# Row statistics in one pass, gate products in another space, an earlier load and refitted planner times in a gated convolution and token-MLP kernel

## The chip, the cores and the metric

The kernel runs on one core of a Trainium2 chip. The metric is the device time of one launch in microseconds, as the median of several runs. The core has five engines with queues of their own: PE (matmul; PEld is its weight load), DVE (vector), ACT (scalar), POOL, and SP, which here only issues DMAs. Each queue runs in order; semaphores connect them.

## The reference

The inputs are bf16; S = 2048 rows, D = 640 channels, F = 1536 hidden units.

```python
x = A_q
g = sigmoid((x * gate_w).sum(-1, keepdims=True))
# A: short convolution (4 taps) over k, product with v, long causal convolution by FFT
k_shift = sum over t of k_pad[:, t:t+S, :] * shift_k[:, ks-1-t]
kv = k_shift * v
y = irfft(rfft(kv, 2S) * rfft(ssm_k, 2S))[:S] + kv * ssm_D
a = x * y
# B: layernorm over D without weights, MLP over the row (token) axis
h = (x - mean) / sqrt(var + 1e-5)
u = gelu_tanh(einsum("bsd,sf->bdf", h, w1) + b1)
b = (einsum("bdf,fs->bds", u, w2) + b2) transposed back
return g * a + (1 - g) * b
```

## The kernel before

The long convolution is done as transforms by matmul. A 2048-row sequence is held as `[128, 2, 4, 640]` halves: four residues p modulo 4, two blocks kt (`hk = 2h + kt` counts the four quarters of 512 rows). The forward transforms of the filter (`transp` through PE into `wT`, then `fwd` with the table `FTB`, results evacuated by ACT into `C[0]`, `C[1]`) and of kv (into `C[2]`, `C[3]`) are followed by additions and subtractions on DVE (`mixing`) that combine the residues. DVE then multiplies spectra (`cross`, `y1`, `product`), some sums being made by accumulating DMAs issued from POOL (`v1mix`, `acc_dma`). `invmix` undoes the mixing, and `inverse(h, Z)` transforms back with the table `GTB`, which is `FTB` transposed by four DMA transposes. ACT scales the inverse by the gate `gg` into `cgb`, DVE multiplies it by q (`q_hi` for the upper half of the rows, `q_lo` for the lower), adds it to `O1` and SP stores the rows.

The MLP has two products. `X` holds all of q, normalised in place: per row tile two `bn_stats` over 320 columns and one `bn_aggr` (`ln_tile`), then `ln_apply(hk)` for each quarter: on POOL var + 1e-5 into `vtmp` and its power of -0.5 into `rstd`, on DVE four `tensor_scalar` that subtract the mean and multiply. The first product ("m1", 12 hidden tiles ft of 32 matmuls each, weights in `ring`) fills PE wherever the convolution leaves it free and ends in a Gelu on ACT into `GT`. The second ("m2", 16 row tiles of 24 matmuls, weights in `W2`, an alias of `ring`) is the filler of the later part; ACT puts it into `O1`, which lies on `X`.

The gate is recovered from the normalised rows: DVE multiplies X by `gate_w` (`gq`, two row tiles each, three buffers), ACT sums each row (`gsum`, a copy into `junk` with an accumulator), and a few 16-column operations on DVE put mean and deviation back, `vtmp * rstd` being the standard deviation.

Buffers share space by hand: `gq` and `junk` lie on `KF` (the taps of the short convolution, read by PE until the fourth quarter's kv), `kp1` (one of two buffers for the permuted k that the k transposes read) lies on `GTB`, `q_hi` on `C[0]`, `q_lo` on half of `C[1]`, `cgb` on `FTB`, `W2` on `ring`.

The order of all work is set by a list scheduler in the file (`_Sched`). Each operation is added with an engine, an estimated duration, and a priority (its place in the program unless given; lower goes first; m1 and m2 have the highest numbers and so fill). The scheduler simulates the engines with these estimates, takes on each engine the ready operation of lowest number, and the order so found is what each engine's queue is given. PSUM has four tiles; at most three go to the convolution and two to the MLP. DMAs are modelled as one channel with 2 us of latency. An operation added with `.after` may not start ahead of another's start in this simulation. At run time only the order remains, with waits on semaphores wherever a dependence crosses engines.

L293 is the matmul helper, L617 `tensor_tensor`, L627 and L628 `tensor_scalar`, L655 `activation`, L724 the k copy, L845 and L847 the statistics, L260, L262 and L267 the DMA helper (transposing, accumulating, plain).

Of the kernel before, what the change touches and what calls it, by code (L numbers as in the profile page):

```python
# [322 lines left out]
class _Sched:  # L323
# [58 lines left out]
    def run(self):  # L382
# [24 lines left out]
        t = 0.0  # L407
# [4 lines left out]
        while started < n:  # L412
            while frees and frees[0][0] <= t:
                _, sl, cls = heapq.heappop(frees)
                nfree.append(sl)
                held[cls] -= 1
            nxt = []
            progress = False
            for e in engs:
                while pend[e] and pend[e][0][0] <= t:  # L420
                    _, p, i = heapq.heappop(pend[e])
                    heapq.heappush(ready[e], (p, i))
                if free[e] > t:
                    nxt.append(free[e])
                    continue
                skipped = []
                pick = None
                while ready[e]:
                    p, i = heapq.heappop(ready[e])
                    op = ops[i]  # L430
                    if op.vt is not None and op.vt.slot is None:
                        c = op.vt.cls
                        if not nfree or held.get(c, 0) >= self.limit.get(c, 99):
                            skipped.append((p, i))
                            continue
                    pick = op
                    break
                for s in skipped:
                    heapq.heappush(ready[e], s)
                if pick is None:  # L440
                    if pend[e]:
                        nxt.append(pend[e][0][0])
                    continue
                op = pick
                progress = True
                started += 1
                if op.vt is not None and op.vt.slot is None:
                    nfree.sort()
                    op.vt.slot = nfree.pop(0)
                    held[op.vt.cls] = held.get(op.vt.cls, 0) + 1  # L450
                op.start = t
                if e in ("SP", "QA") or op.lat < 0:
                    issue = 0.1
                    s = max(t + issue, dma_free)
                    dma_free = s + op.dur
                    op.end = dma_free + 2.0
                    free[e] = t + issue
                else:
                    op.end = t + op.dur
                    free[e] = op.end  # L460
                order.append(op)
                if op.vt is not None:
                    op.vt.left -= 1
                    if op.vt.left == 0:
                        heapq.heappush(frees, (op.end + 0.05, op.vt.slot, op.vt.cls))
                for s in op.asucc:
                    avail[s] = max(avail[s], op.start)
                    s.ndep -= 1
                    if s.ndep == 0:
                        heapq.heappush(pend[s.eng], (avail[s], s.prio, s.idx))  # L470
                for s in op.succ:
                    lat = 0.08 if s.eng == e else 0.15
                    if e == "PE" and s.eng == "PE":
                        lat = 0.0
                    avail[s] = max(avail[s], op.end + lat)
                    s.ndep -= 1
                    if s.ndep == 0:
                        heapq.heappush(pend[s.eng], (avail[s], s.prio, s.idx))
                nxt.append(free[e])
            if not progress:  # L480
                c = [x for x in nxt if x > t]
                if frees:
                    c.append(frees[0][0])
                assert c, "schedule stuck: " + str([(o.name, o.eng, o.ndep) for o in ops if not hasattr(o, "end")][:12])
                t = min(c)
# [19 lines left out]
def _build(nc, A_q, A_k, A_v, A_shift_k, A_ssm_k, A_ssm_D, B_x, B_w1, B_b1, B_w2, B_b2, gate_w, out):  # L505
# [10 lines left out]
    with ExitStack() as es:  # L516
# [32 lines left out]
            return bass.AP(tensor=h, offset=p0 * row + off, ap=[[row, pn]] + [list(d) for d in dims])  # L549

        gwb = alloc("gwb", [128, D], BF16)
        Drow = alloc("Drow", [1, D], BF16)
        ident = alloc("ident", [128, 128], BF16)
        KF = alloc("KF", [128, NG, 7, 32], BF16)
        cw = alloc("cw", [128, NG, 7], BF16)
        m32 = alloc("m32", [128, 32], BF16)
# [4 lines left out]
        vtmp = alloc("vtmp", [128, 16], F32)  # L561
# [18 lines left out]
        dif = alloc("dif", [128, 128], I32, at=base_of(SS) + 64 + 1024)  # L580
        dif2 = alloc("dif2", [128, 32], I32, at=base_of(SS) + 64 + 1536)
        KT = [alloc(f"KT{i}", [128, NG, KTW], BF16) for i in range(2)]
        gq = [alloc(f"gq{i}", [128, 2, D], BF16, at=base_of(KF) + 2560 * i) for i in range(3)]
        junk = alloc("junk", [128, D], BF16, at=base_of(KF) + 7680)
        ssm = alloc("ssm", [128, ND, S], BF16, at=base_of(C[3]))
        wT = alloc("wT", [128, 4, 4, D], BF16, at=base_of(C[2]))
        vkv0 = alloc("vkv0", [128, 2, 4, D], BF16, at=base_of(C[3]))
# [8 lines left out]
        O1 = alloc("O1", [128, 4, 4, D], BF16, at=base_of(X))  # L596
        tm = [alloc(f"tm{i}", [128, 2, 4, D], BF16, at=E_base + 2 * SL * 2 * i) for i in range(2)]
        q_lo = alloc("q_lo", [128, 2, 4, D], BF16, at=base_of(C[1]) + 2 * SL * 2)
        q_hi = alloc("q_hi", [128, 2, 4, D], BF16, at=base_of(C[0]))
        cgb = [alloc(f"cgb{i}", [128, 2, D], BF16, at=base_of(FTB) + 2560 * i) for i in range(3)]  # L600

        def n_of(ap):
# [3 lines left out]
            return n  # L606

        def dve_dur(n, mode):
            return n / {1: 960.0, 2: 1920.0, 4: 3840.0}[mode] + (0.1 if mode == 4 else 0.16)

        def act_dur(n, nap=0):
            return n / 1200.0 + 0.19 + 0.09 * nap

        def tt(eng, o, a, b, op, mode=2, prio=None):
            n = n_of(o)
# [49 lines left out]
            return SC.add(eng, 0.2, lambda s: T.op(eng, lambda e: e.memset(ap, val), [], [ap]), [], [ap], prio=prio)  # L665

        def mms(vt, items, prio=None, name="mm"):
            dur = sum(max(n_of(r) / 2400.0, 0.06) for _, _, r, _, _ in items)
            rd = []
            for _, l, r, _, _ in items:  # L670
                rd += [l, r]
# [48 lines left out]
        def k_turn(hk):  # L720
            o, i = kp[hk % 2], kn[hk % 2]
            ov = o[:, :, :].rearrange("p g (q c) -> p g q c", q=4)
            iv = V(i, 0, [[32, NG], [D, 4], [1, 32]])
            SC.add("DVE", 0.85, lambda s: T.op("DVE", lambda e: e.tensor_copy(ov, iv), [i[:, :, :]], [o[:, :, :]]), [i[:, :, :]], [o[:, :, :]], prio=0, name="kperm")  # L724
# [115 lines left out]
        def ln_tile(hk, p):  # L840
            t = 4 * hk + p
            xs = X[:, hk, p, :]
            for ci in range(2):
                o, i = stats[:, t, 6 * ci:6 * ci + 6], xs[:, 320 * ci:320 * ci + 320]
                SC.add("DVE", 0.46, (lambda o, i: lambda s: T.op("DVE", lambda e: e.bn_stats(o, i), [i], [o]))(o, i), [i], [o])  # L845
            o, i = mv[:, t, :], stats[:, t, :]
            SC.add("DVE", 0.2, (lambda o, i: lambda s: T.op("DVE", lambda e: e.bn_aggr(o, i), [i], [o]))(o, i), [i], [o])  # L847
# [84 lines left out]
        for ft in range(FT):  # L932
# [12 lines left out]
                mms(vt, items, prio=10 ** 6 + 4 * ft + hk, name="m1")  # L945
            g_ = act(GT[:, ft, :].rearrange("p (a b) -> p a b", a=2), two, ACT.Gelu_apprx_tanh, bias=cc[:, 16 + ft:17 + ft], vt=vt, prio=0, name="gelu")
            if ft == 0:
                act(junk[:, :], gwb[:, :], ACT.Copy, acc=gws[:, :], name="gws").after.add(g_)
# [12 lines left out]
        tt("DVE", gpre[:, :], gpre[:, :], gth[:, :], ALU.add, mode=1, prio=0)  # L961
        act(gth[:, :], gpre[:, :], ACT.Tanh, scale=0.5, prio=0)
# [4 lines left out]
        def w2_load(hk):  # L967
            for a in range(2):
                dma(W2[hk % 2][:, 6 * a:6 * a + 6, :], dr(B_w2, a * 6 * 128 * S + 512 * hk, [[S, 128], [128 * S, 6], [1, 512]]), 128 * 6144)

        for p in range(4):
            dma(GTB[:, p, :, :, :, :].rearrange("q a b c d -> q (a b c) d"), FTB[:, p, :, :, :, :].rearrange("q a b c d -> q (a b c) d"), 128 * 2048, rate=200.0, transpose=True, prio=10 ** 5)

        HORD = (2, 3, 0, 1)
        for n_, hk in enumerate(HORD):
            w2_load_at = n_
            W2h = W2[n_ % 2]
            for a in range(2):
                dma(W2h[:, 6 * a:6 * a + 6, :], dr(B_w2, a * 6 * 128 * S + 512 * hk, [[S, 128], [128 * S, 6], [1, 512]]), 128 * 6144)
            for p in range(4):  # L980
                vt = _VT("mlp")
                t = 4 * hk + p
# [170 lines left out]
```

## Time and profile before

| | |
|---|---|
| median of 3 runs | 198.19 us (197.91 to 199.74) |
| the profiled execution | 197.93 us, span 196.1 us, granted clock 0.996 |
| PE busy | 177.4 us, 1403 matmuls |
| DVE busy | 177.0 us, 196 instructions |
| ACT busy | 118.5 us, 187 instructions |
| POOL busy | 28.6 us, 30 instructions |
| DMA | 37.62 MB, mean 192 GB/s |

The span runs from the first to the last instruction of the profiled execution. Rows of a timeline begin with start and duration in microseconds, then engine, line, operation, output and inputs, and in brackets how long the engine stood idle ahead of it and what ended that. SPq is the time in which SP's queue issued a DMA. Rows with bars are groups: busy time, mean nanoseconds of one, idle time ahead.

### The profile page before, as it was taken

The numbers are of one execution on the slowest core, as the hardware profiler recorded it, in microseconds if no ns is written. First come the engines' busy times: TensorE is split into PE (matmuls) and PEld (weight loads), VectorE is DVE, ScalarE is ACT, GpSimd is POOL, SyncE is SP. The second block draws the span as 40 slices with busy tenths as digits, with TensorE's granted clock in tenths as the row PEclk, the third lists the DMA queues.
The fourth block names the chain that finished last, engine by engine and source line by source line (L and its number), as shares of the span: only waits on it lengthen the run. The fifth ranks groups of instructions, "written<-read, shape, count | busy, mean of one in ns | idle before, by whom it ended". The sixth has DMA issues, their size and how long they took to land.

```text
span 196.1 us, 3370 instructions
## 1 busy us (share of the span) xinstructions
PE 177.4 (90%) x1403; PEld 131.4 (67%) x1403; DVE 177.0 (90%) x196; ACT 118.5 (60%) x187; POOL 28.6 (15%) x30
## 2 busy tenths in 40 slices
PE   0759987999999999999999999999999979997890
PEld 0546564468767787777777778888888867775560
DVE  7996998799999179999999879999999599989994
ACT  4798967997749793799796413131313117664471
POOL 2629802500005400000000000040400000000000
PEclk9999999999999999999999999999999999999998
DMA  5999999994999999960053008029999960222034
GB/s 162 331 409 379 364 209 253 310 417 143 165 276 265 227 199 191 258 202 0 3 185 135 3 24 282 15 64 232 234 305 231 383 269 5 91 76 101 3 107 160
DMA packets 36719, 37.62 MB, mean 192 GB/s; under 512 B 15579, under 2 KB 32608, under 8 KB 36704
## 3 DMA queue, kind: packets, MB, share of 16 engines
q1 hardware_dynamic: 34464, 32.15, 54.4%
q0 software_dynamic: 2176, 5.24, 14.4%
q8 instruction: 11, 0.18, 0.4%
q14 instruction: 4, 0.03, 0.0%
q10 hardware_dynamic: 64, 0.01, 0.0%
HBM read 25.87 MB, written 2.62 MB: 145 GB/s over the span
## 4 chain that ended last, share of the span: by engine, by line
PE 67%; DVE 16%; DMA 9%; ACT 3%; POOL 2%; issue 2%; SPq 0%; DVEq 0%
PE pp L293 67%; DMA kn<-in_A_k_dram 5%; DMA X<-in_A_q_dram 4%; DVE kp L724 3%; DVE stats L845 2%; DVE C L617 2%; DVE SS L617 2%; DVE X L628 2%; ACT ksh L655 2%; DVE vkv L617 1%; DVE cgb L617 1%; DVE O L617 1%; POOL rstd L617 1%; POOL vtmp L627 1%; ACT cgb L655 1%
## 5 line engine op out<-in xcount | busy, mean ns | idle before, releaser
L293 PE MATMUL pp<-X,ring 128*128 128x320 bf16 x384 | 55.5, 299 | 1.6 <-DVE X L628 1.6
L617 DVE TENSOR_TENSOR C<-C 128x2560 bf16<-128x2560 bf16 (+1 forms) x28 | 48.9, 1773 | 8.3 <-ACT C L655 5.5
L293 PE MATMUL pp<-GT,W 128*128 128x320 bf16 x384 | 52.8, 299 | 1.1 <-ACT O L655 1.1
L293 PEld LDWEIGHTS pp<-GT,W 128*128 128x128 bf16 x384 | 43.5, 113 | 10.0 <-issue 1.4
L293 PEld LDWEIGHTS pp<-X,ring 128*128 128x128 bf16 x384 | 36.6, 98 | 17.6 <-DVE X L628 2.0
L655 ACT ACTIVATE C<-pp 128x640 bf16<-128x640 f32 x64 | 39.9, 723 | 5.5 <-PE pp L293 5.2
L655 ACT ACTIVATE O<-pp,c,omg 128x640 bf16<-128x640 f32 (+1 forms) x17 | 14.5, 853 | 37.9 <-PE pp L293 37.9
L617 DVE TENSOR_TENSOR tm<-C,C 128x2560 bf16<-128x2560 bf16 (+1 forms) x12 | 22.8, 1930 | 0.0
L262 POOL DMA_DIRECT2D C<-C x6 | 7.5, 1406 | 90.1 <-DVE C L617 90.1
L293 PE MATMUL pp<-wT,FTB 128*128 128x320 bf16 x128 | 20.2, 314 | 0.4 <-ACT wT L655 0.4
L655 ACT ACTIVATE GT<-pp,cc 128x640 bf16<-128x640 f32 x12 | 9.5, 792 | 14.6 <-PE pp L293 14.5
L617 DVE TENSOR_TENSOR C<-tm 128x1280 bf16<-128x1280 bf16 (+1 forms) x16 | 18.0, 1154 | 0.1
L293 PEld LDWEIGHTS pp<-wT,FTB 128*128 128x128 bf16 x128 | 11.9, 102 | 7.8 <-ACT C L655 2.3
L655 ACT ACTIVATE cgb<-pp,gg 128x640 bf16<-128x640 f32 x16 | 12.6, 794 | 6.4 <-PE pp L293 3.3
L293 PE MATMUL pp<-C,GTB 128*128 128x320 bf16 x96 | 13.7, 299 | 2.2 <-DVE C L617 2.2
L293 PE MATMUL pp<-ident,ssm 128*128 128x128 bf16 x80 | 8.4, 265 | 6.2 <-DVE pint L617 5.3
L845 DVE BATCH_NORM_STATS2 stats<-X 128x6 f32<-128x320 bf16 x32 | 13.5, 460 | 0.4 <-DMA X<-in_A_q_dram 0.4
L293 PEld LDWEIGHTS pp<-C,GTB 128*128 128x128 bf16 x96 | 9.2, 98 | 6.4 <-DVE C L617 2.5
L655 ACT ACTIVATE junk<-gq 128x640 bf16<-128x640 bf16 x16 | 11.8, 737 | 0.5
L293 PEld LDWEIGHTS pp<-ident,ssm 128*128 128x128 bf16 x80 | 6.5, 127 | 8.0 <-DMA ssm<-in_A_ssm_k_dram 5.3
L655 ACT ACTIVATE wT<-pp 128x640 bf16<-128x640 f32 x16 | 10.2, 711 | 2.6 <-PE pp L293 2.6
L655 ACT ACTIVATE ksh<-pp 128x1024 bf16<-128x1024 f32 (+1 forms) x12 | 9.6, 893 | 3.2 <-PE pp L293 3.2
(63 smaller groups left out, 176.6 us busy)
## 6 DMA issues: line engine op xcount, KB each, us to landing
ring<-in_B_w_dram SPq DMA_DIRECT2D x12, 512.0 KB, 10.9
W<-in_B_w_dram SPq DMA_DIRECT2D x8, 768.0 KB, 6.9
C<-C POOLq DMA_DIRECT2D x6, 640.0 KB, 11.3
ssm<-in_A_ssm_k_dram SPq DMA_DIRECT2D x4, 640.0 KB, 9.0
X<-in_A_q_dram SPq DMA_DIRECT2D x4, 640.0 KB, 9.3
kn<-in_A_k_dram SPq DMA_DIRECT2D x4, 640.0 KB, 8.5
out_dram<-O SPq DMA_DIRECT2D x7, 320.0 KB, 2.3
vkv<-in_A_v_dram SPq DMA_DIRECT2D x2, 640.0 KB, 4.7
```

The costliest lines, as they stand in the source:

```text
L262: ins = engobj.dma_start(out_ap, in_ap, accum_op=ALU.add, max_dma_last_dim=2560)
L293: ins = self.nc.tensor.matmul(ps_ap, lhsT=lhsT, rhs=rhs, start=start, stop=stop, skip_group_check=True)
L617: return SC.add(eng, d, lambda s: T.op(eng, lambda e: e.tensor_tensor(o, a, b, op), [a, b], [o]), [a, b], [o], prio=prio, name="tt")
L627: return e.tensor_scalar(o, a, s1, None, op0=op0)
L628: return e.tensor_scalar(o, a, s1, s2, op0=op0, op1=op1)
L655: return T.op("ACT", lambda e: e.activation(o, src, func, **kw), rr + [src], ww)
L724: SC.add("DVE", 0.85, lambda s: T.op("DVE", lambda e: e.tensor_copy(ov, iv), [i[:, :, :]], [o[:, :, :]]), [i[:, :, :]], [o[:, :, :]], prio ...
L845: SC.add("DVE", 0.46, (lambda o, i: lambda s: T.op("DVE", lambda e: e.bn_stats(o, i), [i], [o]))(o, i), [i], [o])
```

## The change

- `ln_apply` runs once, behind all sixteen row tiles' statistics: one addition and one power over 16 columns on POOL, the product of the two there as well (`sd`, which replaces `vtmp` and the DVE multiply of the gate chain), then sixteen `tensor_scalar` on DVE.
- `gq` moves from KF's space to GTB's; `junk` goes, the row sums write in place. The transposes that fill `GTB` so come behind the last row sum.
- `Drow` and `ident` change places so that `Drow` and `KF` are adjacent; `q_hi` lies on the two, and its load stands ahead of the W2 loads in the program.
- The load of `q_lo` is held behind the last W2 load in the simulated order. `product(A0[0])` comes behind `inverse(1)` instead of ahead of `invmix` of `Z1`.
- The scheduler's durations are fitted anew: DVE, ACT, matmul, statistics and k copy, and 3 us more for DMAs issued from POOL.

```diff
-                    op.end = dma_free + 2.0
+                    op.end = dma_free + 2.0 + (3.0 if e == "POOL" else 0.0)
...
         gwb = alloc("gwb", [128, D], BF16)
+        ident = alloc("ident", [128, 128], BF16)
         Drow = alloc("Drow", [1, D], BF16)
-        ident = alloc("ident", [128, 128], BF16)
         KF = alloc("KF", [128, NG, 7, 32], BF16)
...
-        gq = [alloc(f"gq{i}", [128, 2, D], BF16, at=base_of(KF) + 2560 * i) for i in range(3)]
-        junk = alloc("junk", [128, D], BF16, at=base_of(KF) + 7680)
+        gq = [alloc(f"gq{i}", [128, 2, D], BF16, at=base_of(GTB) + 2560 * i) for i in range(3)]
...
-        q_hi = alloc("q_hi", [128, 2, 4, D], BF16, at=base_of(C[0]))
+        q_hi = alloc("q_hi", [128, 2, 4, D], BF16, at=base_of(Drow))
...
-            return n / {1: 960.0, 2: 1920.0, 4: 3840.0}[mode] + (0.1 if mode == 4 else 0.16)
+            return n / {1: 960.0, 2: 1920.0, 4: 3840.0}[mode] + (0.04 if mode == 4 else 0.08)
...
-            return n / 1200.0 + 0.19 + 0.09 * nap
+            return n / 1200.0 + 0.09 + 0.05 * nap
...
-            dur = sum(max(n_of(r) / 2400.0, 0.06) for _, _, r, _, _ in items)
+            dur = sum(max(n_of(r) / 2400.0 + 0.0025, 0.056) for _, _, r, _, _ in items)
...
(the k copy: 0.85 becomes 0.75; bn_stats: 0.46 becomes 0.38; bn_aggr: 0.2 becomes 0.12)
...
-        def ln_apply(hk):
-            r = slice(4 * hk, 4 * hk + 4)
-            ts("POOL", vtmp[:, r], mv[:, r, 1], 1e-5, None, ALU.add)
-            tt("POOL", rstd[:, r], vtmp[:, r], V(cst, 1, [[0, 4]]), ALU.pow)
-            for p in range(4):
-                t = 4 * hk + p
-                ts("DVE", X[:, hk, p, :], X[:, hk, p, :], mv[:, t, 0:1], rstd[:, t:t + 1], ALU.subtract, ALU.mult, mode=4, extra=0.17)
+        def ln_apply():
+            ts("POOL", sd[:, :], mv[:, :, 1], 1e-5, None, ALU.add)
+            tt("POOL", rstd[:, :], sd[:, :], V(cst, 1, [[0, 16]]), ALU.pow)
+            tt("POOL", sd[:, :], sd[:, :], rstd[:, :], ALU.mult)
+            for t in range(16):
+                xs = X[:, t // 4, t % 4, :]
+                ts("DVE", xs, xs, mv[:, t, 0:1], rstd[:, t:t + 1], ALU.subtract, ALU.mult, mode=4, extra=0.16)
...
                     for p in range(4):
                         ln_tile(hk, p)
-                    ln_apply(hk)
+                ln_apply()
...
-                        act(junk[:, :], gb[:, b, :], ACT.Copy, acc=gacc[:, t:t + 1], name="gsum")
-
-        tt("DVE", gth[:, :], vtmp[:, :], rstd[:, :], ALU.mult, mode=1, prio=0)
-        tt("DVE", gth[:, :], gth[:, :], gacc[:, :], ALU.mult, mode=1, prio=0)
+                        act(gb[:, b, :], gb[:, b, :], ACT.Copy, acc=gacc[:, t:t + 1], name="gsum")
+
+        tt("DVE", gth[:, :], sd[:, :], gacc[:, :], ALU.mult, mode=1, prio=0)
...
+        for kt in range(2):
+            dma(q_hi[:, kt, :, :], dr(A_q, (1024 + 512 * kt) * D, [[4 * D, 128], [1, 4 * D]]), 128 * 5120)
         for n_, hk in enumerate(HORD):
...
-                dma(W2h[:, 6 * a:6 * a + 6, :], ...)
+                w2last = dma(W2h[:, 6 * a:6 * a + 6, :], ...)
...
         y1(1)
-        for kt in range(2):
-            dma(q_hi[:, kt, :, :], dr(A_q, (1024 + 512 * kt) * D, [[4 * D, 128], [1, 4 * D]]), 128 * 5120)
-        product(A0[0], A0[0], V0[0])
         Z1 = invmix(A1[0], A1[1], C3a, None, None)
         inverse(1, Z1)
...
         for kt in range(2):
-            dma(q_lo[:, kt, :, :], dr(A_q, 512 * kt * D, [[4 * D, 128], [1, 4 * D]]), 128 * 5120)
+            dma(q_lo[:, kt, :, :], dr(A_q, 512 * kt * D, [[4 * D, 128], [1, 4 * D]]), 128 * 5120).after.add(w2last)
+        product(A0[0], A0[0], V0[0])
         product(A0[1], A0[1], V0[1])
```

More of the change, by code (lines that the diff above doesn't have):

```diff
@@ L560, in _build @@
         rstd = alloc("rstd", [128, 16], F32)
-        vtmp = alloc("vtmp", [128, 16], F32)
+        sd = alloc("sd", [128, 16], F32)
         gpre = alloc("gpre", [128, 16], F32)
@@ L598, in _build @@
         q_lo = alloc("q_lo", [128, 2, 4, D], BF16, at=base_of(C[1]) + 2 * SL * 2)
-        q_hi = alloc("q_hi", [128, 2, 4, D], BF16, at=base_of(C[0]))
+        q_hi = alloc("q_hi", [128, 2, 4, D], BF16, at=base_of(Drow))
+        assert base_of(KF) == base_of(Drow) + 1280
         cgb = [alloc(f"cgb{i}", [128, 2, D], BF16, at=base_of(FTB) + 2560 * i) for i in range(3)]
@@ L723, in k_turn @@
             iv = V(i, 0, [[32, NG], [D, 4], [1, 32]])
-            SC.add("DVE", 0.85, lambda s: T.op("DVE", lambda e: e.tensor_copy(ov, iv), [i[:, :, :]], [o[:, :, :]]), [i[:, :, :]], [o[:, :, :]], prio=0, name="kperm")
+            SC.add("DVE", 0.75, lambda s: T.op("DVE", lambda e: e.tensor_copy(ov, iv), [i[:, :, :]], [o[:, :, :]]), [i[:, :, :]], [o[:, :, :]], prio=0, name="kperm")
             c0 = 16 + 128 * (hk % 2)
@@ L844, in ln_tile @@
                 o, i = stats[:, t, 6 * ci:6 * ci + 6], xs[:, 320 * ci:320 * ci + 320]
-                SC.add("DVE", 0.46, (lambda o, i: lambda s: T.op("DVE", lambda e: e.bn_stats(o, i), [i], [o]))(o, i), [i], [o])
+                SC.add("DVE", 0.38, (lambda o, i: lambda s: T.op("DVE", lambda e: e.bn_stats(o, i), [i], [o]))(o, i), [i], [o])
             o, i = mv[:, t, :], stats[:, t, :]
-            SC.add("DVE", 0.2, (lambda o, i: lambda s: T.op("DVE", lambda e: e.bn_aggr(o, i), [i], [o]))(o, i), [i], [o])
-        def ln_apply(hk):
-            r = slice(4 * hk, 4 * hk + 4)
-            ts("POOL", vtmp[:, r], mv[:, r, 1], 1e-5, None, ALU.add)
-            tt("POOL", rstd[:, r], vtmp[:, r], V(cst, 1, [[0, 4]]), ALU.pow)
-            for p in range(4):
-                t = 4 * hk + p
-                ts("DVE", X[:, hk, p, :], X[:, hk, p, :], mv[:, t, 0:1], rstd[:, t:t + 1], ALU.subtract, ALU.mult, mode=4, extra=0.17)
+            SC.add("DVE", 0.12, (lambda o, i: lambda s: T.op("DVE", lambda e: e.bn_aggr(o, i), [i], [o]))(o, i), [i], [o])
+        def ln_apply():
[5 more added lines that the diff above has]
+                ts("DVE", xs, xs, mv[:, t, 0:1], rstd[:, t:t + 1], ALU.subtract, ALU.mult, mode=4, extra=0.16)
         srcW = lambda h: (lambda kt, p, ci: wT[:, 2 * h + kt, p, 320 * ci:320 * ci + 320])
@@ L947, in _build @@
             if ft == 0:
-                act(junk[:, :], gwb[:, :], ACT.Copy, acc=gws[:, :], name="gws").after.add(g_)
+                act(gq[2][:, 0, :], gwb[:, :], ACT.Copy, acc=gws[:, :], name="gws").after.add(g_)
             if ft in (1, 3, 5, 7):
@@ L965, in _build @@
         tt("DVE", c2[:, :].rearrange("p (a b) -> p a b", a=4), omg[:, :].rearrange("p (a b) -> p a b", a=4), b2f, ALU.mult, mode=1, prio=0)
-        def w2_load(hk):
-            for a in range(2):
-                dma(W2[hk % 2][:, 6 * a:6 * a + 6, :], dr(B_w2, a * 6 * 128 * S + 512 * hk, [[S, 128], [128 * S, 6], [1, 512]]), 128 * 6144)
         for p in range(4):
@@ L974, in _build @@
         HORD = (2, 3, 0, 1)
+        for kt in range(2):
+            dma(q_hi[:, kt, :, :], dr(A_q, (1024 + 512 * kt) * D, [[4 * D, 128], [1, 4 * D]]), 128 * 5120)
         for n_, hk in enumerate(HORD):
-            w2_load_at = n_
             W2h = W2[n_ % 2]
             for a in range(2):
-                dma(W2h[:, 6 * a:6 * a + 6, :], dr(B_w2, a * 6 * 128 * S + 512 * hk, [[S, 128], [128 * S, 6], [1, 512]]), 128 * 6144)
+                w2last = dma(W2h[:, 6 * a:6 * a + 6, :], dr(B_w2, a * 6 * 128 * S + 512 * hk, [[S, 128], [128 * S, 6], [1, 512]]), 128 * 6144)
             for p in range(4):
```

## The prediction

> **What bounds the kernel now.** I read the page's busy shares first, then the chain that ended last, then the stretch after the front, then each engine's timeline.
>
> ```profile
> PE 177.4 (90%) x1403; PEld 131.4 (67%) x1403; DVE 177.0 (90%) x196; ACT 118.5 (60%) x187; POOL 28.6 (15%) x30
> PE   0759987999999999999999999999999979997890
> ACT  4798967997749793799796413131313117664471
> 56.08 100.97 PE pp L293 x782
> 40.63:191.32 150.69, 147.08 (x1178) 112.57 (x1175) 139.29 (x106) 84.65 (x134) 9.93 (x8) 1.00 0.61 162
> ```
>
> PE and DVE look equally full, but the chain is PE for 101 us on end, in all for 67% of the span: PE's own queue sets the end. The last row, its columns being span, PE, PEld, DVE, ACT and POOL, is the stretch from 40.63 us to PE's last matmul: of 150.69 us PE is busy 147.08, so only 3.6 us are idle there. Whatever the change wins comes out of those 3.6 us or out of the 40 us ahead of them, where PE's row shows 0 to 8 tenths in places.
>
> ```profile
> 23.78 0.99 PE L293 MATMUL pp<-X,ring 128*128 128x320 bf16 x6
> 25.09 0.44 PE L293 MATMUL pp<-X,ring 128*128 128x320 bf16 x2 [0.32 <-DVE X L628]
> ...
> 26.74 1.25 PE L293 MATMUL pp<-X,ring 128*128 128x320 bf16 x8
> 27.82 1.00 PE L293 MATMUL pp<-ident,ssm 128*128 128x128 bf16 x15
> ...
> 31.49 1.42 PE L293 MATMUL pp<-X,ring 128*128 128x320 bf16 x8 [0.76 <-DVE X L628]
> ...
> 39.37 1.43 PE L293 MATMUL pp<-X,ring 128*128 128x320 bf16 x8 [0.49 <-DVE X L628]
> 40.63 1.79 PE L293 MATMUL pp<-wT,FTB 128*128 128x320 bf16 x12
> ...
> 43.34 1.79 PE L293 MATMUL pp<-wT,FTB 128*128 128x320 bf16 x12
> ...
> 68.86 3.42 PE L293 MATMUL pp<-KF,KT 128*128 128x128 bf16 x64
> ...
> 117.76 39.28 PE L293 MATMUL pp<-GT,W 128*128 128x320 bf16 x288
> 158.11 4.51 PE L293 MATMUL pp<-GT,W 128*128 128x320 bf16 x32 [1.07 <-ACT O L655]
> ...
> 182.28 4.63 PE L293 MATMUL pp<-C,GTB 128*128 128x320 bf16 x32 [2.22 <-DVE C L617]
> ```
>
> A dense 320-column matmul costs 39.28/288 = 0.136 us. In front, PE stands at the head of its queue for the normalised X three times (0.32, 0.76, 0.49 us). Late, it waits 1.07 us for a free PSUM tile and 2.22 us for the last spectrum from DVE; those two are most of the 3.6.
>
> **The change part by part.** First the statistics. Before, one normalising pass per quarter waits for its own power on POOL:
>
> ```profile
> 16.14 0.83 DVE L845 BATCH_NORM_STATS2 stats<-X 128x6 f32<-128x320 bf16 x2
> ...
> 16.99 0.43 DVE L845 BATCH_NORM_STATS2 stats<-X 128x6 f32<-128x320 bf16 x1
> 19.04 1.16 DVE L628 TENSOR_SCALAR X<-X,mv,rstd 128x640 bf16<-128x640 bf16 x3 [1.61 <-POOL rstd L617]
> 20.33 4.35 DVE L724 COPY kp<-kn 128x2560 bf16<-128x2560 bf16 x1
> 24.60 0.79 DVE L628 TENSOR_SCALAR X<-X,mv,rstd 128x640 bf16<-128x640 bf16 x2
> 25.31 0.81 DVE L724 COPY kp<-kn 128x2560 bf16<-128x2560 bf16 x1
> ...
> 34.44 1.48 DVE L617 TENSOR_TENSOR SS<-C 128x2560 bf16<-128x2560 bf16 x1
> ...
> 38.78 1.51 DVE L628 TENSOR_SCALAR X<-X,mv,rstd 128x640 bf16<-128x640 bf16 x4
> 19.97 4.03 POOL L617 TENSOR_TENSOR KF<-cw,m 128x2240 bf16<-128x2240 bf16 x1
> 29.51 0.23 POOL L627 TENSOR_SCALAR vtmp<-mv 128x4 f32<-128x4 f32 x1 [5.51 <-DVE mv L847]
> 29.82 1.04 POOL L617 TENSOR_TENSOR rstd<-vtmp,cst 128x4 f32<-128x4 f32 x1
> 36.12 1.41 POOL L627 TENSOR_SCALAR vtmp<-mv 128x4 f32<-128x4 f32 x1 [5.27 <-DVE mv L847]
> 17.49 7.26 ACT L655 ACTIVATE C<-pp 128x640 bf16<-128x640 f32 x12 [0.16 <-PE pp L293]
> ```
>
> The 32 statistics and 16 applications stay. Four `vtmp` and four powers become one of each over 16 columns, a POOL multiply is added, one small DVE multiply (0.18 us) goes. The k copy takes 4.35 us where its neighbour takes 0.81, and it ends when POOL's KF product ends (19.97 + 4.03 = 24.0): the two hold each other off. With the powers gone from between POOL's two KF products (the first powers ran right ahead of the one at 19.97, at 4 us a product), the second KF product should run from 17.6 to 21.6.
>
> When is X ready afterwards? A tile is two statistics and an aggregate, from 16.14 to 16.99, so 0.85 us; nine are done at 17.0. Seven more take 6.0, the two copies 0.74 each; the statistics end at about 23.5, the second copy at 24.2. Then POOL: 0.2 for the addition, the power, 0.25 for the multiply, 0.3 between engines. The trace has no power of 128x16. From below it is the 1.04 us of 128x4, if the cost is per call; from above four times that, 4.2, if it is per element. A cheap POOL operation of the same four columns takes 0.23, so 0.81 of the 1.04 belongs to the power itself, and I take it as per element: 0.23 + 4 x 0.81 = 3.5. The power so ends at 28 and the sixteen applications of 0.365 us start at about 28.5: X's first quarter is ready at 30.0 (27.5 with the power at 1.04, 30.7 at 4.2), the last at 34.4. Before, the first was ready at 25.3, the last at 40.2. **The first quarter comes almost 5 us later, the last 6 us earlier.**
>
> The rule that speaks against this part is in the Trainium skill, "SBUF — State Buffer", section "Who interferes with whom": POOL and a DVE instruction with two SBUF inputs that meets a POOL read exclude each other for a whole instruction. The long k copy agrees with it, and so does the last `vtmp` row, 1.41 us against 0.23. By the rule a filler that DVE starts while POOL waits holds the three POOL operations up, or a 3.5 us power holds DVE up.
>
> From the rows alone: the filler would be a mixing addition of 1.48 us (the row of 34.44), so from zero to 1.4 us more ahead of X. I take zero, since the copy before the power already ends about when POOL starts, and keep 1.4 for the range.
>
> What PE does with it: the order is fixed before the run, with the power entered at 0.33 us (16/500 + 0.3 in `tt`), so the plan has X's first quarter ready at about 26 to 27 and puts the first X matmuls near there, as before at 23.78. PE then stands from about 27 to 30. What is hidden behind it: ACT, which takes 7.26/12 = 0.6 us for each evacuated tile and is the limit of that stretch anyway, is drained after three tiles and then stands as well.
>
> Now the sum. At 40.63 before, PE had done all transposes of the filter, the `wT` matmuls but 24 (the rows of 40.63 and 43.34), and 32 of X (the five rows ahead), with 150.7 us to go of which 147.1 busy. After, at 30.0, it lacks against that state 40 `wT` matmuls, 32 of X and some five tiles of transposes (25 small matmuls at 1.00/15, less their modelled end, 0.06), 72 x 0.136 + 25 x 0.06 = 11.3 us. From then on X is there for filling. PE's end = 30.0 + 11.3 + 147.1 = 188.4, plus what is still lost: in the ACT-limited rest of the front I allow 0.5 us, late 0.3 to 0.5. That is **189.3 against 191.3**.
>
> The last quarter's wait of 0.49 and the late 1.07 and 2.22 must be gone for that. The 2.22 is DVE being late, and DVE gets ahead:
>
> ```profile
> 69.90 2.83 DVE L617 TENSOR_TENSOR C<-C 128x5120 bf16<-128x5120 bf16 x1 [5.28 <-ACT C L655]
> ...
> 154.25 1.49 DVE L617 TENSOR_TENSOR C<-C 128x2560 bf16<-128x2560 bf16 x1 [2.57 <-DMA C<-C]
> 155.66 2.82 DVE L617 TENSOR_TENSOR tm<-C,SS 128x5120 bf16<-128x5120 bf16 x1
> L617 DVE TENSOR_TENSOR gq<-X,gwb 128x1280 bf16<-128x1280 bf16 x8 | 6.5, 820 | 0.0
> L655 ACT ACTIVATE junk<-gq 128x640 bf16<-128x640 bf16 x16 | 11.8, 737 | 0.5
> L655 ACT ACTIVATION_READ_ACCUMULATOR junk<-gq 128x1 f32 x16 | 3.1, 194 | 0.0
> 46.78 6.93 SPq L260 DMA_TRANSPOSE KT<-kp  x2
> ...
> 56.41 10.31 SPq L260 DMA_TRANSPOSE GTB<-FTB  x3
> ...
> 98.44 32.92 SPq L267 DMA_DIRECT2D W<-in_B_w_dram  x6
> DMA to landing us min/median/max: 4.6/6.9/13.5
> ```
>
> Three parts feed it. The gate products lay in KF's space and waited for its last reader (68.86 + 3.42 = 72.3); in GTB's space they wait only for the k transposes (issued by 53.7), so three of them, 2.2 us, fit into the 5.28 us in which DVE waits for ACT. The space has three buffers, and the next ones need ACT's sums of 0.93 us each: 2.2 is the part I count. The k copy's stall is worth 3.5 us on DVE. The 2.57 us wait for an accumulating transfer is known to the planner now (3 us more for POOL's transfers), and the product of A0[0], whose half was spent ahead of the first inverse, now ranks behind it like the one of 155.66, so that there is more to fill the wait with; I count half, 1.3. Together 7 us against a deficit of 2.2, less the 3 us of new waiting for the power, leaves the end to PE. If that cover fails, up to 2.2 comes back.
>
> The rest costs nothing by these covers: `q_hi` in the dead KF and Drow space can load any time from 72 us and is wanted once the inverse starts, after 158.11; `q_lo`, behind the last W load, is wanted after PE's 182.28; in-place sums replace `junk` one for one; the fitted costs change only the order, and their gain or loss is in the two allowances, from 0 to 2 us late (what before has, 3.6, is the upper end).
>
> One part has a price of its own. The four inverse-table transposes, 10.31/3 = 3.4 us of SP each, cannot start until the last gate sum has left GTB's space; before, three were issued at 56.41 and one ahead of the first k transposes. SP takes 13.8 us for four, and queued behind are the W loads for the second MLP product. A half of W lands 4.6 us after its issue at the least (the last row, from the answer on the tile W). I take it as hidden: ACT's digits 7, 9, 3 and 7 from 64 to 84 leave 1.4 slices of 4.9 us, seven sums, so the sixteen should end near 100; W's first pair goes out near 97 and is needed at 117.76 less 2, the second is needed 13 us after that and can be issued at 116. Nothing else is late on SP; at the front one transpose less lets SP issue those of k some microseconds earlier, which I count only as cover.
>
> The tail after PE (4.8 us) I leave, less 0.3 if a half tile of the MLP ends the run. Sum: 196.1 - 2.0 - 0.3 = 193.8 of span; the profiled execution's 197.93 lies 1.8 above its span, so **195.6**. It lies 0.26 under the median of the runs, 198.19, against which I reckon the chances: 1%, 2 us, is about what a measurement of this kernel can tell from no change.
>
> **The rivals.**
>
> *The power is cheap, or PE does not stand.* With 1.04 us X's first quarter is at 27.5 and the sum gives 193.1; if the planned order has transposes ahead of X there, another 1 us less. For it: POOL's 2240-column product costs 4.03 us, so columns as such are cheap. Against it: 0.81 us of four columns' power. Time 191.5 to 194.
>
> *The front eats the gain.* The mixing filler and the power exclude each other (1.4 us), and half of the late 3.6 us returns in a new place, since order is static and transfers land when they like: 195.6 + 1.4 + 1.6 = 198.6, no measurable change. For it: the front was already waiting for POOL three times. Here too belongs that the change does not do what it says: the order hardly moves late, and the 2.22 us stay.
>
> *Slower: the transposes stand ahead of W.* The planner puts a gate sum at 640/1200 + 0.09 = 0.62 us, the trace shows 0.74 and 0.19 more for the accumulator, so over sixteen the plan is some 4 us early. If it puts the four transposes on SP ahead of W's first pair, that pair is issued 13.8 us after the last sum and its first half lands 4.6 us later, while PE wants it at 115.8: it costs nothing up to a last sum at 97.4 and then microsecond for microsecond. With the last sum at 102 it is 4.6 to 5 us: 200.4. If the last sum is so late that W's first pair is out, W's second pair meets the same queue: a sum at 111 gives 111 + 13.8 + 4.6 = 129.4 against 128.8, a loss of 1 to 2.
>
> **How the numbers follow.** My forecast (194 to 197.2) has 0.38; the cheap front 0.19; the eaten gain 0.26; slower 0.17. The range reaches from inside the cheap front, 191.8, to inside the slow case, 200.2, leaving about 0.1 at each end. Faster by over 1% means under 196.2: all of the cheap front, four fifths of the forecast, 0.50. Slower, over 200.2: most of the last rival and a little of the third, 0.17. Within 1%: 0.33.
>
> **What would show it.** Right: one power of about 3.5 us on POOL near 24 to 28; a k copy of 0.8 to 1.3 us; all X applications in one row from about 28.5 to 34; PE idle for X once for some 3 us and not again; gate products from about 60; transposes on SP at about 100 with W's first pair ahead; PE's last matmul at 189. Wrong: a power near 1 us; PE waiting for W near 115 or 128; PE waiting for DVE after 150; DVE idle for ACT at 65 as long as before. The step I trust least is where the plan places the first X matmuls.

## The result and the profile after

The changed kernel takes 193.04 us in the median against 198.19 shown ahead of the prediction; with a fourth run of the kernel before, whose median is then 198.91, the ratio is 0.970, 95% interval 0.963 to 0.977. Runs of the kernel before fall on two levels, near 198.0 us and, at a granted clock lower by about 0.01, near 199.7, which makes the intervals wide; two disturbed executions stand aside, one of the changed kernel (270.78 us at a clock of 0.675; the other three lie within 0.3 us, their median is 192.99) and the profiled one of the first experiment (651.14 us). The profiled execution took 192.82 us, its span is 191.0: 5.1 us less.

The busy row of PE from the page, and two stretches of the kernel after: from 40.95 us to PE's last matmul, then to the end. The columns are stretch, length, busy time of PE, PEld, DVE, ACT and POOL, then granted clock, DMA share and GB/s.

```profile
PE   0749989999899999999999999999999999999993
40.95:187.89 146.94, 146.10 (x1170) 110.69 (x1167) 136.37 (x106) 81.45 (x130) 9.94 (x8) 1.00 0.62 167
187.89:191.00 3.11, 0.00 (x1) 0.00 (x0) 0.33 (x1) 0.62 (x1) 0.00 (x0) 1.00 0.27 96
```

The same answer on the kernel before, for what follows PE's last matmul there:

```profile
191.32:196.10 4.78, 0.00 (x0) 0.00 (x0) 2.15 (x5) 0.79 (x1) 0.00 (x0) 0.84 0.44 157
```

PE ends at 187.9 instead of 191.3 (3.4 us), and what follows takes 3.11 us instead of 4.78 (1.7 us). PE's idle time after some 41 us fell from 3.6 to 0.84. The rest of PE's gain lies in front; here is its timeline after.

```profile
14.36 10.92 PE L293 MATMUL pp<-wT,FTB 128*128 128x320 bf16 x64 [0.43 <-ACT wT L655]
25.25 0.44 PE L293 MATMUL pp<-ident,ssm 128*128 128x128 bf16 x5
25.85 3.96 PE L293 MATMUL pp<-ident,ssm 128*128 128x128 bf16 x35 [0.15 <-ACT C L655]
29.93 1.31 PE L293 MATMUL pp<-wT,FTB 128*128 128x320 bf16 x8
31.09 1.25 PE L293 MATMUL pp<-X,ring 128*128 128x320 bf16 x8
32.17 4.01 PE L293 MATMUL pp<-wT,FTB 128*128 128x320 bf16 x28
36.02 1.25 PE L293 MATMUL pp<-X,ring 128*128 128x320 bf16 x8
37.10 4.01 PE L293 MATMUL pp<-wT,FTB 128*128 128x320 bf16 x28
40.95 1.25 PE L293 MATMUL pp<-X,ring 128*128 128x320 bf16 x8
...
51.78 3.75 PE L293 MATMUL pp<-vkv,FTB 128*128 128x320 bf16 x26 [0.79 <-DVE vkv L617]
...
177.92 9.97 PE L293 MATMUL pp<-GT,W 128*128 128x320 bf16 x72
```

All 64 matmuls of the first transform run in one row where X broke them after 56; all eight tiles of transposes for the second transform precede the first X matmul; the second transform runs in rows of 28. At 40.95 all 128 `wT` matmuls and 16 of X are done; before, at 40.63, it was 104 and 32. That is 8 matmuls ahead, 0.3 us later: the busy time left for PE is 146.10 us instead of 147.08, 1.0 less, so 0.7 us net. With 2.8 us less idle time later it makes the 3.4. The run now ends in an MLP tile (x72), behind which only a half tile is evacuated, added and stored.

POOL and DVE around the statistics, and DVE and SP later, from the timelines of the kernel after:

```profile
25.62 1.39 POOL L627 TENSOR_SCALAR sd<-mv 128x16 f32<-128x16 f32 x1 [4.06 <-DVE mv L847]
27.09 2.94 POOL L617 TENSOR_TENSOR rstd<-sd,cst 128x16 f32<-128x16 f32 x1
23.20 1.48 DVE L617 TENSOR_TENSOR SS<-C 128x2560 bf16<-128x2560 bf16 x1
...
25.45 1.44 DVE L617 TENSOR_TENSOR C<-C 128x2560 bf16<-128x2560 bf16 x1
30.07 5.79 DVE L628 TENSOR_SCALAR X<-X,mv,rstd 128x640 bf16<-128x640 bf16 x16 [3.19 <-POOL rstd L617]
...
63.59 2.83 DVE L617 TENSOR_TENSOR C<-C 128x5120 bf16<-128x5120 bf16 x1 [1.06 <-ACT C L655]
87.77 9.11 SPq L260 DMA_TRANSPOSE GTB<-FTB  x4
98.53 46.01 SPq L267 DMA_DIRECT2D W<-in_B_w_dram  x8
```

The power takes 2.94 us and the addition ahead of it 1.39; X's first quarter is ready at 30.07 + 4 x 0.36 = 31.5. DVE waits for ACT 1.06 us instead of 5.28, and the table's transposes are through on SP before W's first pair.

### The profile page after: what moved, and what is told of

It reads as the page before. It is cut to its first block, busy times and chain, and to the rows that moved or that the text cites. A ratio compares the mean times of both kernels' runs of the same rounds, so it can differ in the third digit from the quotient of the medians.

```text
span 191.0 us, 3354 instructions
## 1 busy us (share of the span) xinstructions
PE 177.8 (93%) x1403; PEld 131.1 (69%) x1403; DVE 173.1 (91%) x195; ACT 116.8 (61%) x187; POOL 29.6 (16%) x25
## 3 DMA queue, kind: packets, MB, share of 16 engines
HBM read 25.87 MB, written 2.62 MB: 149 GB/s over the span
## 4 chain that ended last, share of the span: by engine, by line
PE 71%; DVE 19%; DMA 4%; POOL 2%; issue 2%; SPq 0%; ACT 0%; DVEq 0%
PE pp L293 71%; DVE stats L845 6%; DMA X<-in_A_q_dram 4%; DVE X L628 3%; DVE SS L617 3%; DVE C L617 2%; DVE kp L724 2%; POOL rstd L617 2%; DVE vkv L617 1%; DVE mv L847 1%; POOL sd L627 1%; SPq L267 0%; ACT O L655 0%; DVE O L617 0%; DVEq L187 0%
## 5 line engine op out<-in xcount | busy, mean ns | idle before, releaser
L293 PE MATMUL pp<-X,ring 128*128 128x320 bf16 x384 | 53.8, 299 | 0.0
L293 PEld LDWEIGHTS pp<-X,ring 128*128 128x128 bf16 x384 | 37.4, 98 | 14.6 <-issue 0.2
L617 DVE TENSOR_TENSOR O<-cgb,O 128x1280 bf16<-128x1280 bf16 (+2 forms) x10 | 6.8, 690 | 6.4 <-ACT O L655 6.3
L655 ACT ACTIVATE gq<-gq 128x640 bf16<-128x640 bf16 x16 | 11.8, 757 | 0.6 <-DVE gq L617 0.6
L617 DVE TENSOR_TENSOR tm<-C,SS 128x5120 bf16<-128x5120 bf16 x4 | 11.1, 2817 | 0.0
```

The lines of the kernel that those rows point to most:

```text
L293: ins = self.nc.tensor.matmul(ps_ap, lhsT=lhsT, rhs=rhs, start=start, stop=stop, skip_group_check=True)
L617: return SC.add(eng, d, lambda s: T.op(eng, lambda e: e.tensor_tensor(o, a, b, op), [a, b], [o]), [a, b], [o], prio=prio, name="tt")
L655: return T.op("ACT", lambda e: e.activation(o, src, func, **kw), rr + [src], ww)
```

## The experiments

Each is an edit of the changed kernel ("a") or of the kernel before ("b"); times are medians.

**Whose is the gain?** First all the planner's old durations in the changed kernel, and only the new ones in the kernel before.

```diff
# a_old_costs (b_new_costs is the same edit the other way, on the kernel before)
-  dma_free + 2.0 + (3.0 if e == "POOL" else 0.0)      +  dma_free + 2.0
-  DVE  ... + (0.04 if mode == 4 else 0.08)            +  ... + (0.1 if mode == 4 else 0.16)
-  ACT  n / 1200.0 + 0.09 + 0.05 * nap                 +  n / 1200.0 + 0.19 + 0.09 * nap
-  PE   n / 2400.0 + 0.0025, at least 0.056            +  n / 2400.0, at least 0.06
-  k copy 0.75, bn_stats 0.38, bn_aggr 0.12            +  0.85, 0.46, 0.2
-  the application's extra 0.16                        +  0.17
```

> The changed kernel with all the planner's old durations. If the gain is the planner's (theory P: fitted times order DVE so that the last spectrum is in time and the MLP ends the run), most of the 5 us goes: 196 to 198.5, with PE idle over 2 us after 41 us. If it is the structure's (theory S: one normalising pass, gate products early, late loads moved), it stays: 192.5 to 194.5.

Measured: 198.39 us (ratio to the kernel before 0.997, 0.994 to 1.001). Its waits can't be read from the profiled execution, so the expected idle time of PE is not shown; its order can: PE ends as in the kernel before, with 48 MLP matmuls and then two inverses.

> The kernel before with the fitted durations alone. P: 193.5 to 195.5, tail after PE's last matmul near 3.1 us. S: 196.5 to 199, tail 4.8 us as before.

Measured: 193.43 us (0.973, 0.968 to 0.978). PE's last rows there:

```profile
178.50 4.51 PE L293 MATMUL pp<-SS,GTB 128*128 128x320 bf16 x32
182.84 5.60 PE L293 MATMUL pp<-GT,W 128*128 128x320 bf16 x40
```

Theory P holds from both sides, and S falls: without the durations the structural edits give nothing that can be told from the kernel before; the durations alone give all but 0.4 us of the gain, the end in an MLP tile included.

**Which durations?** Each alone put back in the changed kernel.

```diff
# a_old_act
-            return n / 1200.0 + 0.09 + 0.05 * nap
+            return n / 1200.0 + 0.19 + 0.09 * nap
```

> The changed kernel with ACT's old durations alone (0.1 us too much for each evacuated tile). Theory F (the plan of the front and of the 41 to 85 us stretch goes wrong because ACT, the limit there, is planned too slow, so PE is given MLP matmuls between transforms and ACT then really stands): 195 to 198, PE's long rows of transform matmuls broken by X. Theory D (it is DVE's durations, through the late spectra): 192.5 to 193.8.

Measured: 198.49 us, 5.4 more than the changed kernel. PE's timeline in front, one row later on, the granted clock in tenths (40 slices of 4.9 us, 9 is 0.9 or more), and the stretch from 40.95 us:

```profile
25.73 1.57 PE L293 MATMUL pp<-ident,ssm 128*128 128x128 bf16 x15 [0.15 <-ACT C L655]
30.67 2.04 PE L293 MATMUL pp<-X,ring 128*128 128x320 bf16 x8 [3.36 <-DVE X L628]
32.50 1.27 PE L293 MATMUL pp<-ident,ssm 128*128 128x128 bf16 x10
...
36.71 2.34 PE L293 MATMUL pp<-wT,FTB 128*128 128x320 bf16 x16
38.88 1.25 PE L293 MATMUL pp<-X,ring 128*128 128x320 bf16 x8
39.97 1.79 PE L293 MATMUL pp<-wT,FTB 128*128 128x320 bf16 x12
...
151.09 12.69 PE L293 MATMUL pp<-GT,W 128*128 128x320 bf16 x92 [1.02 <-DMA W<-in_B_w_dram]
PEclk9999996999999999999999999999999999999999
40.95:193.15 152.20, 149.49 (x1194) 113.75 (x1192) 136.47 (x106) 86.98 (x140) 9.93 (x8) 1.00 0.65 169
```

Planned slow, ACT seems to leave PE time in the middle of the transposes. The plan fills it with X, which is not there yet: 3.36 us in which ACT has nothing to evacuate either. From then on the transforms run in rows of 12, with X between. PE ends 5.3 us later than in the changed kernel. Some 3.4 of that is work not done by 40.95 (about 87 `wT` matmuls and 32 of X against 128 and 16), 1.9 is more idle time behind it (2.7 us against 0.84). This is theory F.

The stall is followed by a second loss. The granted clock, 1.00 up to it, is 0.55 from 30.67 to 33.50 and 0.86 from there to 36.70, and PE is busy all that time: eight X matmuls take 2.04 us at 30.67 and 1.25 at 38.88. I estimate some 1.7 us from it (0.45 x 2.83 + 0.14 x 3.20); they fall into the 3.4. In the changed kernel, where PE doesn't stand there, the clock is 1.00 over the whole front. That the stall brings the lower clock about was not tried by itself.

```diff
# a_old_dve: dve_dur, k copy, bn_stats, bn_aggr, the application's extra as before
-            ... + (0.04 if mode == 4 else 0.08)
+            ... + (0.1 if mode == 4 else 0.16)
```

> The changed kernel with DVE's old durations alone (0.08 us too much per operation, statistics too). D: 195 to 198, PE waiting for DVE after 150 us and the tail 4.8 us again, because the plan puts the last inverse after the last MLP tile. F: 192.5 to 193.8.

Measured: 196.45 us, 3.4 more. The profiled execution is the longest of four, 196.85 us, and its span is 4.1 us longer than the changed kernel's. Two rows of ACT at the start, DVE's first k copy, PE's first `wT` row and last row, and what follows PE's last matmul:

```profile
6.22 0.70 ACT L655 ACTIVATE wT<-pp 128x640 bf16<-128x640 f32 x1 [2.62 <-PE pp L293]
6.94 1.28 ACT L655 ACT_TABLE_LOAD   x1
...
21.54 3.55 DVE L724 COPY kp<-kn 128x2560 bf16<-128x2560 bf16 x1 [2.38 <-DMA kn<-in_A_k_dram]
16.03 11.61 PE L293 MATMUL pp<-wT,FTB 128*128 128x320 bf16 x64
...
185.72 4.51 PE L293 MATMUL pp<-SS,GTB 128*128 128x320 bf16 x32
190.23:195.10 4.87, 0.00 (x0) 0.00 (x0) 2.16 (x5) 0.79 (x1) 0.00 (x0) 0.98 0.40 138
```

The end is as D said: the plan thinks the last spectrum late, spends the MLP first, ends in the inverse, and the tail is 4.87 us instead of 3.11 (1.8 of the 4.1). The wait of PE for DVE late, which D also named, isn't there. The other 2.3 us are PE's, and they lie in front, where I had expected nothing: the plan thinks the table's arguments late, so ACT takes a copy ahead of the sines, waits 2.62 us for it and loads a table once more, and the first transform starts at 16.03 instead of 14.36. The k copy is queued so early that DVE waits for its data and then, 3.55 us instead of 0.8, for POOL. So F and D are both right in what they claim, in different places, and wrong in that each ruled out the other; their two costs, 5.4 and 3.4, don't add up (together 5.4).

```diff
# a_old_mm
-            dur = sum(max(n_of(r) / 2400.0 + 0.0025, 0.056) ...)
+            dur = sum(max(n_of(r) / 2400.0, 0.06) ...)
# a_old_dmapool
-                    op.end = dma_free + 2.0 + (3.0 if e == "POOL" else 0.0)
+                    op.end = dma_free + 2.0
```

> The changed kernel with the old matmul duration alone (2.4 us too little over 960 matmuls). Both theories: 192.7 to 194; above 195 would say that PE's own duration sets the order late.

Measured: 192.66 us; the fitted matmul duration gains nothing, in this order it costs 0.4.

> The changed kernel without the planner's 3 us more for POOL's transfers. If this is what saves the 2.6 us wait of DVE for an accumulating transfer: that wait returns, and with DVE well ahead PE does not notice: 192.7 to 193.5. If the late spectra hang on it: 194.5 to 196.

Measured: 193.05 us, the same as the changed kernel; DVE's wait for the transfer does not return either.

```diff
# b_new_act: the kernel before with ACT's durations alone
-            return n / 1200.0 + 0.19 + 0.09 * nap
+            return n / 1200.0 + 0.09 + 0.05 * nap
```

> The kernel before with ACT's fitted durations alone. If ACT's share is as large from this side (undoing it in the changed kernel cost 5.4 us): 194 to 196. If the durations only work together: 196.5 to 199, with the tail of 4.8 us or a wait of PE that ACT alone doesn't mend.

Measured: 193.59 us (0.975, 0.970 to 0.980): this one line is worth almost the whole change, better than I expected. It keeps one of the old late waits and the old end, the last row being an inverse:

```profile
156.83 3.42 PE L293 MATMUL pp<-GT,W 128*128 128x320 bf16 x24 [1.07 <-ACT O L655]
...
183.35 4.51 PE L293 MATMUL pp<-SS,GTB 128*128 128x320 bf16 x32
```

**What the structural edits do on the new plan.** Undone one at a time.

```diff
# a_quarters
-        def ln_apply():             # 16 columns at once, behind all statistics
+        def ln_apply(hk):           # 4 columns, behind each quarter's; sd by quarters too
```

> The changed kernel with one normalising pass per quarter again (power and product on POOL by quarters). If the single pass won in front, by an uninterrupted ACT and no wait of PE for X: 193.6 to 195.5, PE waiting for X two or three times again. If X's later first quarter was a cost (as I had reckoned), 191 to 192.8.

Measured: 194.20 us, 1.2 more, so the single pass is a gain, but not by the waits for X that I had named. PE's waits of that kernel up to 80, and a row of ACT:

```profile
27.03 1.25 PE L293 MATMUL pp<-X,ring 128*128 128x320 bf16 x8
...
42.58 4.33 PE L293 MATMUL pp<-KF,KT 128*128 128x128 bf16 x80 [1.15 <-ACT C L655]
...
54.62 3.75 PE L293 MATMUL pp<-vkv,FTB 128*128 128x320 bf16 x26 [1.62 <-DVE vkv L617]
...
76.71 0.72 PE L293 MATMUL pp<-kv,FTB 128*128 128x320 bf16 x4 [0.59 <-ACT GT L655]
39.75 1.28 ACT L655 ACT_TABLE_LOAD   x1
```

X comes early and PE never waits for it. But then the first hidden tile is done near 40, and ACT takes it, with a table to load, ahead of the transform's last evacuations: PE waits 1.15 us for ACT (the kernel before with the new durations has the same wait at 43.02), later 1.62 instead of 0.79 for DVE, and 0.59 for a Gelu of ACT. So X's late first quarter seems to keep the MLP out of the way there.

```diff
# a_gq_in_KF
-        gq = [alloc(f"gq{i}", [128, 2, D], BF16, at=base_of(GTB) + 2560 * i) for i in range(3)]
+        gq = [alloc(f"gq{i}", [128, 2, D], BF16, at=base_of(KF) + 2560 * i) for i in range(3)]
```

> The changed kernel with the gate products in the taps' space again (the sums still in place). If the early gate products were needed to get DVE ahead: DVE idle for ACT near 62 goes from 1.1 to 3 us or more, the last spectrum comes late, 194.5 to 196. If DVE had slack to spare anyway: 192.7 to 193.5, only the first inverse moving.

Measured: 192.48 us, 0.6 less. DVE's wait for ACT grows as I had reckoned, without a cost, and PE's wait at 51 is gone:

```profile
63.09 2.83 DVE L617 TENSOR_TENSOR C<-C 128x5120 bf16<-128x5120 bf16 x1 [2.54 <-ACT C L655]
50.96 4.06 PE L293 MATMUL pp<-vkv,FTB 128*128 128x320 bf16 x28
```

DVE has slack to spare. Why PE's wait is gone is not a matter of gate products in DVE's way: in the changed kernel the first of them comes at 54.51, behind both products with v (48.10 and 50.24). What stands ahead of these there is a k copy (47.37, 0.82 us), which the plan of `a_gq_in_KF` puts behind the first of them (47.59). So it's another order of DVE; that the move of `gq` as such costs anything is not shown.

```diff
# a_q_hi_late: q_hi on C[0], loaded behind y1; product(A0[0]) ahead of invmix; q_lo not held
+        for kt in range(2): dma(q_hi[:, kt, :, :], ...)
+        product(A0[0], A0[0], V0[0])
         Z1 = invmix(A1[0], A1[1], C3a, None, None)
```

> The changed kernel with the late part as before: q_hi on C[0] and loaded behind y1, the product of A0[0] ahead of the first inverse, q_lo not held. If these carry part of the gain (earlier first inverse): 193.6 to 195. If not (PE's order is the same and DVE is ahead): 192.8 to 193.3.

Measured: 192.93 us: nothing.

**Who holds up the addition?** One DVE operation moved, orders of PE and ACT the same.

```diff
# a_filler_held, in mixing, fine, i == 0
-                tt("DVE", sl(R, i, n), sl(R, i, n), sl(R, 2 + i, n), ALU.subtract)
+                o_ = tt("DVE", sl(R, i, n), sl(R, i, n), sl(R, 2 + i, n), ALU.subtract)
+                o_.after.add(first normalising tensor_scalar)
```

> The changed kernel with one DVE subtraction of the mixing, the one that ran beside POOL's addition and power, held until the normalising pass starts; PE's and ACT's orders are the same. If DVE and POOL exclude each other: POOL's addition takes 0.25 us and not 1.39, X's first quarter is ready 1.1 to 1.3 us earlier (30.3), and since PE reaches X only at 31.1 and ACT is the limit there, the time stays: 192.7 to 193.3. If POOL's 1.39 is its own cost over 16 columns: X's first quarter stays at 31.5. If X's readiness still limits the front, 191.6 to 192.4.

Measured: 192.38 us, its runs between 191.84 and 193.47. POOL's, DVE's and PE's rows of an execution of 191.84:

```profile
25.65 0.27 POOL L627 TENSOR_SCALAR sd<-mv 128x16 f32<-128x16 f32 x1 [4.05 <-DVE mv L849]
26.01 2.94 POOL L617 TENSOR_TENSOR rstd<-sd,cst 128x16 f32<-128x16 f32 x1
28.98 5.79 DVE L628 TENSOR_SCALAR X<-X,mv,rstd 128x640 bf16<-128x640 bf16 x16 [1.18 <-POOL rstd L617]
50.53 4.01 PE L293 MATMUL pp<-vkv,FTB 128*128 128x320 bf16 x28
```

The addition takes 0.27 us and X is ready 1.1 us earlier: DVE's subtraction did hold it up. PE's first X matmul stays at 31.07, yet the time falls by more than I expected in that execution, because DVE, 1.1 us ahead, has the product with v ready when PE comes to it. Over the four runs the gain is not secure: they spread over 1.6 us, and the longest is above the changed kernel's.

```diff
# c_best: a_gq_in_KF and a_old_mm together
```

> The changed kernel with the gate products back on the taps' space and the old matmul duration, each of which alone was 0.4 to 0.5 us faster. If the two add: 191.9 to 192.3. If both are only another draw of the order: 192.3 to 193.3.

Measured: 192.42 us: the two don't add. Four versions now stand at 192.4 to 192.7, some 0.5 us under the changed kernel. In three of them (this one, the gate products on KF, the subtraction held) PE's 0.79 us wait is absent; the old matmul duration keeps it and is as fast, so what separates them is not settled.

## Why the prediction was right, and where it was not

The direction, the bound and the range held; the forecast of 2.6 us was half of the 5.1, and the time lies outside the forecast's own 194 to 197.2, among the times of the first rival. That the direction came out is in part luck: the structural edits, which the sum worked out, measure 198.39 us with the old durations, no change.

- **PE's queue sets the end**: right; the chain of the kernel after is PE for 71% of the span.
- **The end of PE**: 189.3 forecast, 187.9 measured. The failed step is "PE then stands from about 27 to 30". I had taken the place of the first X matmuls over from the old order, "as before at 23.78". The fitted ACT durations moved them behind all transposes and one part of a transform, to 31.09, by when X's first tiles are ready (the applications run from 30.07 on). The stall that I priced at 3 us is real, but belongs to another kernel: with ACT's old durations it is 3.36 us, from 27.3 to 30.7, with the lower clock behind it, which my sum did not have. In the measured kernel the state that the sum compares is reached at 40.95 - 1.0 = 40.0; my sum had it at 30.0 + 11.3 = 41.3. Those 1.3 us are nearly all of PE's miss of 1.4. The two allowances together, 0.8 to 1 us, met 0.84, of which 0.79 is the one wait for DVE at 51.
- **X's first quarter at 30.0**: came at 31.5. The power took 2.94, not 3.5; of the two ends I had the nearer one. The filler, which I set at zero, was charged twice. One mixing addition (23.20, 1.48 us) ran between the last statistics, so that POOL started at 25.62 and not 24.2; the subtraction behind it met POOL's addition, 1.39 us against 0.27. By the rule of the Trainium skill ("SBUF — State Buffer", "Who interferes with whom") one of the two blocks for the other's whole instruction; here the run with the subtraction held shows it, at 1.1 us for X and nothing on PE's first X row. (The long k copy, which the prediction put under the rule for two SBUF inputs, reads one tensor; it met POOL's product all the same.)
- **The tail, less 0.3**: it is less 1.7. The event was right, a half MLP tile as the last work; its size was not worked out. Before, an evacuation, a multiply, additions and stores follow PE (4.78); after, a half evacuation, one addition of 0.33 and a store (3.11).
- **DVE gets ahead by three parts**: it got ahead, but no part was needed by itself. Gate products back in KF's space, the late loads as before, the planner's 3 us taken away: each leaves the time or betters it. With ACT's new durations alone the gate products lie on KF, a k copy still takes 3.06 us, and yet PE doesn't wait for DVE late. What puts DVE ahead is not settled: there the transforms run in long rows, which brings kv and its mixing forward, but with ACT's old durations in the changed kernel they run in short ones and PE doesn't wait for DVE late either.
- **"The fitted costs change only the order, and their gain or loss is in the two allowances"**: this is where the error of judgement sits. I gave the durations at most 2 us and worked out the structure; the durations were the change, ACT's above all.
- **Rivals**: the first, to which I gave 0.19, came true by half of its condition: the power is not cheap, but PE doesn't stand, and the order does have the transposes ahead of X. Its 193.1 came from a power of 1.04 us; that it meets the measured 193.04 is luck. The transposes do stand ahead of W, where I had expected W's first pair: they are out by 96.9 and W starts at 98.53. That cost nothing: the last gate sum is done at 94.2, short of the 97.4 from which I had it cost, four transposes took SP 9.11 us and not 13.8, and PE doesn't wait for W. With ACT's old durations a wait for W of 1.02 us does appear, at 151, not at 115. "The front eats the gain" is what the structural edits did under the old durations (198.39).

## What to carry to other kernels

Where a planner fixes the order, its durations are part of the kernel: fit them to start-to-start spacing in the trace (7.26/12 = 0.605 us for the evacuation that was entered at 0.72), first those of the engine that limits the stretch where fillers are placed, here ACT in front. Filler goes where the plan believes that engine leaves room, so an error of 0.1 us there put fillers into the middle of a transform and cost 5 us. DVE's errors cost 3.4; those of the matmuls and of POOL's transfers cost nothing, though PE is the engine that sets the end. To judge such a change, ask first where the new plan puts each filler, and whether what it needs is ready there.

## What the runs showed of the hardware

The power on POOL is mostly per column: 1.04 us for 4, 2.94 for 16, so about 0.16 a column and 0.4 beside it. POOL's small copy into KT, 0.28 us in the kernel before, took 6.46 us with DVE's subtraction held (34.04 to 40.50): DVE's instructions follow each other without a gap from 28.98 to 40.38 there, and the copy ends just behind the first gap. In the changed kernel it ends at 37.39, likewise just behind a gap of DVE (37.26 to 37.29). That looks as if POOL got its turn only where DVE pauses, but no rule comes of it: with DVE's old durations the same copy took 0.36 us beside the sixteen applications, which follow each other without a gap as well. What decides it stays open; it cost nothing here. POOL's and DVE's rows of the kernel with the subtraction held, then POOL's of the changed kernel, then both engines' with DVE's old durations:

```profile
34.04 6.46 POOL L927 COPY KT<-KT 128x20 bf16<-128x20 bf16 x1 [4.80 <-DMA KT<-kp]
37.50 2.88 DVE L617 TENSOR_TENSOR C<-SS 128x2560 bf16<-128x2560 bf16 x2
40.41 2.90 DVE L617 TENSOR_TENSOR SS<-C 128x2560 bf16<-128x2560 bf16 x2
```

```profile
34.16 3.23 POOL L921 COPY KT<-KT 128x20 bf16<-128x20 bf16 x1 [3.82 <-DMA KT<-kp]
```

```profile
36.44 0.36 POOL L921 COPY KT<-KT 128x20 bf16<-128x20 bf16 x1
36.23 5.79 DVE L628 TENSOR_SCALAR X<-X,mv,rstd 128x640 bf16<-128x640 bf16 x16 [3.18 <-POOL rstd L617]
```
